# Seven half-size products for all tiles of 480 or 512 tokens, summed on in two PSUM banks and read in between

## The chip, the cores and the metric

The kernel runs on one core of a Trainium2 chip. Its engines are TensorE (PE in the profile; its weight loads are PEld), VectorE (DVE), ScalarE (ACT), GpSimd (POOL) and SyncE (SP), which here only issues transfers. The metric is the device time of one execution in microseconds. Three executions before the change took 838.07, 834.65 and 835.58 us: a median of 835.58 us.

## The reference, cut to what matters

An FFT mixer feeds a two-layer MLP. The input x is 8 sequences of 3008 tokens with 256 columns; the MLP is 256 to 2048 to 256.

```python
X = np.fft.rfft(x, axis=1)
Yr = Xr @ w_r - Xi @ w_i + b_r
Yi = Xr @ w_i + Xi @ w_r + b_i
lam = 0.01            # then both parts are shrunk towards 0 by lam
y = np.fft.irfft(Yr + 1j * Yi, n=x.shape[1], axis=1)

h = y @ w_in          # y as 24064 x 256, h 24064 x 2048
r = np.maximum(h, 0.0)
g = s * (r * r) + b
return g @ w_out      # 24064 x 256
```

## The kernel before, in words

**The FFT.** 3008 is taken as 94 x 32 (`N1`, `N2`), and the transform is done by small matmuls in stages: `s1_units` (the DFT over the 94, into the tile u), `s23_units` (the DFT over the 32, the mixing, the shrinking in the tile ring, and the inverse DFT into v) and `s4_units` (the inverse over the 94, into the tile yt, f16, 128 x 2 x 96 x 32). Between the stages the data goes out to DRAM and back in another order (ud, vd, issued on SP). Sequences 0 and 1 are done somewhat differently at the start, when the tables and weights are being loaded. All these stages leave PSUM through the two banks of the pool psf.

**The MLP.** The 24064 tokens are cut into 48 tiles (`_tile_order`): 12 "wide" ones for sequences 0 and 1 (512 or 480 tokens), then for each later sequence five "main" tiles of 512, and for each pair of sequences two "tail" tiles of 512 and 384 for the last 14 of the 94 rows. A tail's tokens are copied out of yt into the tile tail by POOL (L1036). For each tile `first_mm` makes h in 16 slots (`MC`); in each slot two matmuls of 512 columns (dc = 0, 1) fill one half of a two-bank tile psh, and after every second slot a relu (L1122 on ACT, L1124 on DVE) and a square (L1133 on ACT, L1135 on DVE) give a part of g in the tile gt. The sums with s and b come at the end, in the step that leaves PSUM.

**The second product** of a tile, g @ w_out, runs in the 16 slots of the tile after it, between that tile's first products. In `second_mms` it is 4 x 16 matmuls of 256 columns, in two banks of the pool psa, read by two DVE steps of 512 columns (L1234). In `seven_mms` the tile is cut into halves of tokens and of the inner dimension, the right side into halves of columns, and the 2 x 2 block product is done with seven block products instead of eight (Winograd's form): 7 x 16 matmuls of 128 columns. That asks for sums of blocks of w_out, made once (`make_t`, tile T_s), and for four sums of blocks of g for each half q of a tile (`s_op`): sums 1, 2 and 3 on DVE (L1276), sum 4 by an accumulating transfer that POOL issues (L1290). The seven products go to four banks, and nine DVE steps add them up through a tile zz (L1333, L1366). The function `seven` picks the tiles that are done so: 21 of the 48.

**The order of the work** is fixed by hand: every matmul is placed by the slots, and everything else is a "piece" (`later`) whose turn and engine stand in the table `TURNS`, two characters a piece: after how many matmuls it is issued, and on ACT, DVE, SP or POOL. Each engine works through its own queue in that order. `need` asserts that a piece has been issued before the matmul that depends on it; the waiting itself is done by semaphores.

Of the kernel before, what the change touches and what calls it, by code (L numbers as in the profile page):

```python
# [26 lines left out]
    "28292i242d21282g2l2q1w1x2h252i1o2h3e3m423m1k281k1o1o281t1h251k301h1s29202d371j3b251o21243h1s"  # L27
    "2k442l2q2y1c1d1h1g1p1t1w28202d21292t2x3m4a2u32181s1d1h1l1x21395i3y4i3a0w1s181c211k2c193m1e15"
    "1p21216a5u262u0s151g1t1d1h2h2h2q463m5u101g1s0w390x1h1p212l6q663m4y1g2c0l0t0k0o0y0x1t0w3d1x2e"
    "42190p1t1x292i4a4m560g5u0g0k1o0t0s102h1l4d85111l1x2d6i2y4y4e080e0c0k1h0s1s0t1d1d214a265u560c"  # L30
    "260t0w1g2d462m0h0o111k4k0x151h1p3e2a4u42045m0o0w1c0v0x0x191d1x292e3i2q3i0g0o380p3a101k1s3t42"
    "5e4q4y0l1d1x213h2x2d1t011y050c3c0d192d2t39393d350s4q040o0w0x16142k111h3e212d2l3q3e322i141d1c"
    "1m363m142c183m141d1k2w1s1t2h212y2e1h1q1c242p3d1x251w20252h2y1w201t2a1y2l2p1w3d1x271s3l20212f"
    "2129351k1o241w2t1x1y1w2s1w20242h21222h35202s1x251w20202g1x255a282k2l2x1p3i2y1q3i1d353t191h2w"
    "1c1c1l1p23141l1c39222l2r1l1p291k1s2t2035251w2021242d202g1z252h252d2l314e364q3a1c241l1t181g1w"
    "1l2t7f1l1s281t1t193q4m2u46263i2q0y292h0x11102s0x3l3t3x4q424q4y0d0r08100o1d1r0p0t1x112p141s1x"
    "0x0w25101g2w202l1b1x2h353t4m6i4q5e142l151x1k1u141c111k1o252d254232361y0x390x0o240w191l142t14"
    "1k2l1l1x2l2l462q4q4e0s4u145u18282d362i141g102h1121102k11144q11141l1k2t1w282c1h363e1l1p253p3y"
    "463m4e0j1g200x1a0s5214192o1h1g1g1k1d1k282x464y4i36151d1p1t3p3d41391t3t1p250d220o0y080k140t28"
    "195u182w1l21261x252x4232363a1c1g1l1o1g1m2q1t3e191p181o2g1o2c1p3a2q2y1g1u1d291t2h1o1w28282h25"  # L40
    "2e2028292e2m2l2x1s1w3s1t252f1s1w2x20292j1t25351k1o2o1w2t211u1w2s1t21252p2022393l1x1w3421211o"
    "211s201t234u1x24252p2d3e2q4a2q2h2x183g1515212f101910481y1c2d2n1l1p2h1c2d203g1l2d1x211s241x21"
    "252l2u323e3m1l1k2c3r1h291g2g1d1x1d1s212c301x252h2t323e423i171h1g202h2l193i363y4a3e2a3q460h0p"
    "0t0s1s101534141p1d1l1t313e3e3m3u1c2o0s3q1419212t3i152t11101t131g202c1g2d1x292l31363q3u361k1o"
    "1h4m1l1k1o2d4e191t1d1g211o284l1s211p1x212d2l3a2u3a42143e152c1012181l1c381t2y191o1s1y1w3c1t1x"
    "2d2h2l3x2p3l392h2p1x111024183u0v1l4q1p2g1k1p1x282t361k361l1p1y1o201d1y3a1t1x2g1x221s2529202c"
    "253u242a2e1w281x2l2t1x1x212a1o1w2d242c2t361x36292l1p2w1k1k292r1k1k3s1w2d2r1t1x2p1w1w281t291t"
    "2i252s1s25253420222d391x1w2s1x211s241x2g1w6n321x241x251x3i1y2x311o281l1x1l1z1g1t282p1q2d2n1t"
    "1t2l201k2l1w252t1o281t1w21282k1v252x2129313d4m3u3a3y1k1w151d1c1l1s1g215n1h1g1w1x2x1h2y3a212t"
    "1d1l182o1l3d4h4l4q5i564u111f0k2c0s1l1v11111918290o1d211h142x19181o1s21171x3l3t3x4m5u3u560s2k"  # L50
    "1h1l1042141d14181h15252d362m0o39110s300w1h3l101p141c3g1l212h3p464u463m0s4u181e15241x3m101415"
    "2c103t1c3g11155m1910391d1h1l1c1w2t361d1p1x314a3i3m2y0n1g1s105e185m151d2o191h181g1h1k2d353e1h"
    "1p21292l393x3l312h3d1x0k3q0x4i0c0g0o0o14195u1g2p1h1s1y1o20292y1h1s1w2t1t1u2q1p3i1p1t1s2s1s1w"
    "2s1t1u1y1o221p252d3p2028212525242a2028214u252p1t242s1o1x271s203t1x292n1t1t2d1s1s2h1p2x1t1u1s"
    "281w242c2l2c1y213p2424282d2d1t1x2429215j3q1w201t292d3e2i1p2x1c2k1g1p212j181l1c34262d2j1p1t2t"
    "1w1k2c1s2h291l2829292d24283n2h5p1x2l2l2t3q4m3a2u181k0x19101k1s1t2p131p1o241p1t212u32361u1t31"
    "1c1t1g3s1l393d3l4y4e3m3u191n0s141g1p1z11151x102x102g211l1c1k1t2930282h1r212l3l3t4i423q5a1829"
    "19191g421c1g191g1o1d3d1x3e2q0x2l11101o181d301g2x1d1s241t2h3l3t3y465q56184a154i1c1o2p3e101011"
    "1g112l0w280t0x3q0w0w18192p1l1o282x321d1l2l2t2y3m3m2y0n153d142614321c1g241l1o1p2k1w24313t461t"
    "1x1x214d392d2h313h391p0w3u0w4i0s1h0s10181c4q1k1w1h1t221t252d2y1k1s1s2t1s1u2m1p2m1o1t1s30291t"  # L60
    "24313e1y1x221s21252h1s2h1w1w28292i242d212a2h3120203s20212b211s2820252f2529351o252o1s2p211u1w"
    "2t1t24252w202224253825291s29202821274621252x2x252y321k2h1h1p1g1p1g2k5q1s1x2c1s2t1x2c1x1w2h1t"
    "241v2x3x2h461p1p1t2h4i422i2q101c101c1k192p47191g1s152i252x1d1h1k2o253h3l414u4y46520x1b0w2g14"
    "1p1z11152p1019101t2h1d1c2d1c1g281s2l1b253d3h494y665u46142c1d1l1942151819191k292x1p3m3a0k1h0x"
    "0w380x1c3l0w15191c1o1h1p1x2d364u2e52142q1d221g2o393m1c1g1h281l3p1g2h1d1h1q1h1l1w1k2t1w282l3h"
    "3m1l1x2h2t3e3y3i3m0n1g28141a1c4a1918241l1k1p2g1s20442d2m1p1t2h2t412t312p3h2x352d0o1m0o0y0l2x"
    "0w141w1p4y24281t252e2029393m1p1w1w281s1u2i202q1g251h2p1g1s212p2y3621321k2l1t211g1o2d1s2g242e"
    "212c252e2l2x1x202w1x252f1s1w3h212h2r1x1x2h1s1w2x1t2h1w1y202c2029283929222529202428292p1t2920"
    "2h20274e24242529213e26253l1o201s252d2n1l1l1s3c1i2h2n1l1t35201o2l1w292p1o241l242d242c2d5l1x2l"
    "2x393i4i3i3u1g1x1519181c1o1c2p1h1g1o212h193e2m2u3i253l0t1d0w2g1939414h52564i5a191n0k280o1p23"  # L70
    "0t112918350o1o2115152k101c341c1d1l3d414d4m565q560k241d1t0t1i0s1w0x1d1p212l2t2y3m0o2h110s0w14"
    "143g111t142t1l2d3h3l3y3m4a4i0x1m0w240x3a181g2015191g2c151k1o2x1p1x202c3d4a1p1t2529322q2a2y1c"
    "201d2q1h181t251s2t2124283d3m1t1x292h2x2d2l3t39392p2t11160o1c0w2t1l1s1g212e1w282l3e20242c1t22"
    "2i212o1x1x202d212e26282t25252425242828282p2y292x1t1s3g1s212f1o1w3l202p2z1t1x2h1k1o2t1l291o1w"
    "2t202424282128282s2525242h202o1x27242h21252h262e2029282928292828292h2539292i1s251w2920242t32"
    "2d2p1p2s1t1z1g2h1s351x272929292d1o2c1w2t2h3p1w2g1t1t1w2d202c2d391p3a1q212d1o281x271k2o202x21"
    "271x2d212t1x2d20202h351w2l1x251w20242c213l3p3q3y1x251l201p1z1c2g1o1t1l1r292t2x2x18211o1w1x20"
    "2d2l2025242d2539293i3m32221k1p1s1s1t1t1s1x202s2t2x1t221s1w1x2d20283p3u2d2h1s2k1p1z1k291s2l1p"
    "1z212t3h3h1g211s211s2c2x2x1o1o1p1s313d313i3619201c1l1k1p1o2c1p3e1o252425242524282126292m252i"
    "2122"  # L80
# [77 lines left out]
def kernel(  # L158
# [65 lines left out]
    zpool = ctx.enter_context(tc.tile_pool(name="zp", bufs=1))  # L224
# [273 lines left out]
    b_21 = cpool.tile([P, P], F32, name="b_21")  # L498
# [7 lines left out]
    def make_t(i):  # L506

        if not T_s:
            t_ops.append(later(
                lambda e: nc.vector.tensor_tensor(  # L510
                    out=b_21, in0=bias_bc[:, P:D], in1=bias_bc[:, 0:P], op=ALU.subtract
                ),
                {"dve": 0.2}, needs=bias_ops,
            ))
            T_s.append(x2pool.tile([P, 4, MC // 2, P], F16, name="T_s", tag="x2"))
        t = T_s[0]
        a, b, op = (
            (w_block(0, 1), w_block(0, 0), ALU.subtract),
            (t[:, 0], w_block(1, 1), ALU.subtract),
            (w_block(1, 1), w_block(0, 1), ALU.subtract),  # L520
            (w_block(1, 0), t[:, 1], ALU.add),
        )[i]
        t_ops.append(later(
            lambda e: nc.vector.tensor_tensor(out=t[:, i], in0=a, in1=b, op=op),
            {"dve": 0.6}, needs=t_ops[-1:],
        ))
# [476 lines left out]

    def s4_units(b):

        groups = []
# [4 lines left out]
        def unit(g):  # L1011
# [6 lines left out]
            for j in range(w):  # L1018
                h, k = divmod(n2 + j, HW)
                matmul(  # L1020
                    ps[:, j * N1 : (j + 1) * N1],
                    vs[(b, h)][:, k, ec * P : (ec + 1) * P], C_t[:, 0:N1],
                    start=True, stop=True,
                )

            done = leave_bank(
                yt[:, ec, 0:N1, n2 : n2 + w], ps,
                ps[:, 0 : w * N1].rearrange("p (j n) -> p n j", n=N1), w * N1,
            )
            y_ops[b].append((n2, w, done))  # L1030
            if g == len(groups) - 1 and b >= 2:
                pr, half = divmod(b, 2)
                if half == 0:
                    tails[pr] = tpool.tile([P, DC, 2, 14, N2], F16, name="tail", tag="tail")
                tail_copies[b] = later(
                    lambda e: nc.gpsimd.tensor_copy(  # L1036
                        out=tails[pr][:, :, half], in_=yt[:, :, 80:94, :]
                    ),
                    {"pool": 1.8}, needs=[op for _, _, op in y_ops[b]],
# [489 lines left out]
```

## Time and profile before

| | |
|---|---|
| median of three executions | 835.58 us |
| the profiled execution | 835.52 us |
| its span, first to last instruction | 833.7 us |
| PE busy | 818.9 us, 98% |
| DVE busy | 736.8 us, 88% |
| ACT busy | 702.2 us, 84% |
| POOL busy | 83.4 us, 10% |
| mean granted TensorE clock | 1.000 |
| mean busy share of the DMA engines, 100 to 750 us | 0.53 |

The span is what the profile covers; the execution's own time lies 1.8 us above it. A row of the profile names the source line, the engine, the operation, the tiles written and read, the shapes, how often it ran, the busy time, the mean duration of one, and how long its engine had been idle just before. The durations of neighbouring instructions on one engine overlap, since the end of one runs beside the start of the next, so starts are a better measure of pace than durations. A matmul's 128x512 is 128 rows of output by 512 columns.

### The profile page before, as it was taken

The page shows a single profiled execution, that of the slowest core. Times are in us where ns is not written, and L with a number is a line of the kernel's source. Part 1 is how long each engine was busy: PE and PEld are TensorE (multiplying, and loading weights), DVE is VectorE, ACT ScalarE, POOL GpSimd, SP SyncE. Part 2 cuts the span into 40 slices and gives each one's busy share as a digit, 9 for nine tenths or more (in the row PEclk, how much of TensorE's full clock was granted, in tenths as well). Part 3 has the DMA queues.
Part 4 walks back from the last instruction along what each step waited for, and adds up shares of the span by engine and source line. Part 5 has one row for each costly group of instructions (what it writes and reads, how often), then busy time and mean ns, then how long its engine had stood idle before and what let it go on. Part 6 is the DMA issues. An engine that isn't in the chain of part 4 may idle for free.

```text
span 833.7 us, 19076 instructions
## 1 busy us (share of the span) xinstructions
PE 818.9 (98%) x7662; PEld 598.5 (72%) x7662; DVE 736.8 (88%) x1192; ACT 702.2 (84%) x874; POOL 83.4 (10%) x112
## 2 busy tenths in 40 slices
PE   7999999999999999999999999999999999999997
PEld 6857777777677767777677766777667777767765
DVE  5988989997898999998899979999989989889984
ACT  5989889989798889888889988897879987878774
POOL 4630000100011000110001100110001000001000
PEclk9999999999999999999999999999999999999999
DMA  8963546664547367454656545654566333513222
GB/s 202 182 170 82 120 138 171 131 129 123 173 114 166 85 176 188 108 118 128 176 141 161 112 124 150 150 130 116 129 177 149 72 92 96 140 45 77 74 49 77
DMA packets 114929, 107.14 MB, mean 129 GB/s; under 512 B 11036, under 2 KB 99104, under 8 KB 113496
## 3 DMA queue, kind: packets, MB, share of 16 engines
q1 hardware_dynamic: 100760, 80.55, 33.2%
q0 software_dynamic: 14080, 25.37, 18.5%
q8 instruction: 60, 0.98, 0.5%
q14 instruction: 29, 0.24, 0.1%
HBM read 53.52 MB, written 46.66 MB: 120 GB/s over the span
## 4 chain that ended last, share of the span: by engine, by line
PE 83%; DVE 8%; DMA 5%; ACT 2%; issue 1%; POOL 0%; SPq 0%; DVEq 0%; ACTq 0%; POOLq 0%
PE psh L234 34%; PE psa L234 31%; PE psf L234 17%; DMA ring<-ring 2%; DMA gt<-gt 2%; DVE rt L1124 1%; DMA x<-in_x_dram 1%; PE psm L234 1%; DVE gt L1135 1%; ACT rt L1122 1%; DVE u L297 1%; DVE yt L297 1%; DVE gt L1276 1%; DVE ring L934 0%; POOL x L370 0%
## 5 line engine op out<-in xcount | busy, mean ns | idle before, releaser
L234 PEld LDWEIGHTS <-gt 128*128 128x128 f16 (+1 forms) x3696 | 305.1, 101 | 168.9 <-DMA gt<-gt 1.1
L234 PE MATMUL psh<-yt,w_in 128*128 128x512 f16 (+1 forms) x1344 | 397.2, 378 | 1.5 <-ACT u L297 0.8
L1122 ACT ACTIVATE rt<-psh 128x1024 f32<-128x1024 f32 (+2 forms) x310 | 311.4, 1006 | 63.1 <-PE psh L234 55.7
L234 PE MATMUL psa<-w_out_t,gt 128*128 128x256 f16 (+3 forms) x2448 | 310.1, 253 | 0.7 <-DMA gt<-gt 0.6
L1133 ACT ACTIVATE gt<-rt 128x1024 f16<-128x1024 f32 (+2 forms) x254 | 261.6, 1041 | 11.4 <-DVE rt L1124 8.6
L1135 DVE TENSOR_TENSOR gt<-rt 128x1024 f16<-128x1024 f32 (+2 forms) x130 | 154.3, 1194 | 7.7 <-ACT rt L1122 7.0
L234 PEld LDWEIGHTS <-w_in 128*128 128x128 f16 x1536 | 136.3, 98 | 25.2 <-issue 3.2
L1124 DVE TENSOR_SCALAR rt<-psh 128x1024 f32<-128x1024 f32 (+2 forms) x74 | 88.2, 1193 | 19.9 <-PE psh L234 17.5
L1290 POOL DMA_DIRECT2D gt<-gt x42 | 38.1, 907 | 505.5 <-DVE gt L1276 231.6
L234 PE MATMUL psa<-T_s,gt 128*128 128x128 f16 (+1 forms) x944 | 79.6, 219 | 0.3 <-DVE zz L1333 0.3
L890 DVE TENSOR_TENSOR ring<-psf,s 128x512 f16<-128x512 f32 x84 | 57.6, 686 | 19.9 <-PE psf L234 11.1
L234 PE MATMUL psh<-tail,w_in 128*128 128x512 f16 (+1 forms) x192 | 52.1, 353 | 0.0
L234 PEld LDWEIGHTS <-xf 128*128 128x128 f16 x504 | 47.1, 98 | 4.9 <-DVE xf L850 0.5
L234 PE MATMUL psf<-W_g,xf 128*128 128x256 f16 x336 | 50.4, 273 | 0.0
L297 ACT CAST yt<-psf 128x470 f16<-128x470 f32 (+2 forms) x60 | 37.1, 646 | 4.4 <-PE psf L234 4.2
L1234 DVE SCALAR_TENSOR_TENSOR ost<-psa,s_bc,bias_bc 128x512 f32<-128x512 f32 (+2 forms) x51 | 36.9, 723 | 3.0 <-PE psa L234 2.9
L234 PE MATMUL psf<-x,A_t 94*96 94x512 f16 x102 | 38.9, 382 | 0.3 <-DVE u L297 0.2
L297 ACT CAST xf<-psf 128x512 f16<-128x512 f32 x52 | 30.3, 585 | 10.1 <-PE psf L234 9.9
L1333 DVE SCALAR_TENSOR_TENSOR ost<-psa,s_bc,zz 128x256 f32<-128x256 f32 (+1 forms) x80 | 36.6, 477 | 1.6 <-PE psa L234 0.8
L234 PE MATMUL psf<-C_t,vs 96*128 96x94 f16 (+1 forms) x484 | 37.7, 205 | 0.3 <-ACT yt L297 0.3
L297 ACT CAST u<-psf 96x512 f16<-96x512 f32 x54 | 31.0, 578 | 6.7 <-PE psf L234 5.4
L297 ACT CAST v<-psf 128x512 f16<-128x512 f32 x49 | 28.6, 583 | 9.3 <-PE psf L234 9.1
(121 smaller groups left out, 890.8 us busy)
## 6 DMA issues: line engine op xcount, KB each, us to landing
out_dram<-ost SPq DMA_DIRECT2D x65, 256.0 KB
ud<-u SPq DMA_DIRECT2D x56, 192.0 KB
us<-ud SPq DMA_DIRECT2D x28, 384.0 KB
vd<-v SPq DMA_DIRECT2D x42, 256.0 KB
vs<-vd SPq DMA_DIRECT2D x14, 768.0 KB
x<-in_x_dram POOLq DMA_DIRECT2D x28, 376.0 KB, 6.4
gt<-gt POOLq DMA_DIRECT2D x38, 256.0 KB, 4.0
ring<-ring SPq DMA_DIRECT2D x120, 64.0 KB
```

Of the source, the lines that this page charges most:

```text
L234: return nc.tensor.matmul(out, lhs, rhs, **how)
L297: (nc.scalar.copy if e == "act" else nc.vector.tensor_copy)(out=dst, in_=src)
L890: lambda e: nc.vector.tensor_tensor(out=ring[0][:, i % 4], in0=ps, in1=hold[i // 2][:, i % 2].unsqueeze(1).to_broadcast([P, 2, D]), op=ALU ...
L1122: nc.scalar.activation(out=rt, in_=ps[:, :, 0:w], func=AF.Relu)
L1124: nc.vector.tensor_scalar(out=rt, in0=ps[:, :, 0:w], scalar1=0.0, scalar2=None, op0=ALU.max)
L1133: nc.scalar.activation(out=gt, in_=rr, func=AF.Square)
L1135: nc.vector.tensor_tensor(out=gt, in0=rr, in1=rr, op=ALU.mult)
L1234: nc.vector.scalar_tensor_tensor(out=osts[number % 3][0:size, 0:k], in0=ps[0:size, 0:k], scalar=s_bc[0:size], in1=bias_bc[0:size].unsqueez ...
L1276: nc.vector.tensor_tensor(out=out, in0=a, in1=b, op=op)
L1290: nc.gpsimd.dma_start(out=a12, in_=a11, accum_op=ALU.add)
L1333: nc.vector.scalar_tensor_tensor(out=out, in0=of, scalar=s_bc[0:size], in1=other, op0=ALU.mult, op1=ALU.add)
```

## The change

All tiles of 480 or 512 tokens from tile 4 to tile 45 use `seven_mms`: 39 tiles instead of 21. The rest (tiles 0 to 3, the three of 384 tokens, and the last two) stay with `second_mms`.

Inside `seven_mms` the seven products now use two banks instead of four. Three places of 256 columns are used, called x, v and y: products 0, 4, 5 and 2 all go to x and are added on top of each other, product 1 goes to v, and products 3 and 6 to y; v and y share a bank. The running sums are read between the products by seven DVE steps of 256 columns, a, g, b, c, e, f and h, straight into the output tile ost; zz, `b_21` and the step L1366 are gone. A product that adds to a place must wait until the reading step of that place is done: 4 waits for a, 5 for b, 2 for c, 6 for e, and 3 for g. The order of the products becomes 0, 1, 4, half of 3, 5, the other half of 3, 2, 6, with uneven numbers of matmuls in the slots. Sum 4 may be made on DVE too.

The tile yt of sequences 2 to 7 is kept in 12 blocks of 8 n1, each as 32 x 8, so that a step of `s4_units` writes runs of eight values; its matmuls take 96 columns instead of 94. The rows of a main tile stand in another order for that, and `store` sends them to the same places in DRAM in the same number of pieces for main tiles, and in more and smaller ones for the three tiles of 384. The tail is moved by a transfer issued on SP instead of a copy by POOL. `TURNS` is a new table.

```diff
 TURNS = (
...
 )
...
-    zpool = ctx.enter_context(tc.tile_pool(name="zp", bufs=1))
...
-    b_21 = cpool.tile([P, P], F32, name="b_21")
...
+    def in_blocks(b):
+
+        flat = yts[b].rearrange("p e m n -> p e (m n)")
+        return flat.rearrange("p e (k n r) -> p e k n r", k=12, n=N2)
+
     def s4_units(b):
 
+        cols = N1 if b < 2 else 96
...
+            if b < 2:
+                dst = yt[:, ec, 0:N1, n2 : n2 + w]
+                src = ps[:, 0 : w * N1].rearrange("p (j n) -> p n j", n=N1)
+            else:
+                dst = in_blocks(b)[:, ec, :, n2 : n2 + w].rearrange("p k j r -> p j k r")
+                src = ps[:, 0 : w * 96].rearrange("p (j k r) -> p j k r", j=w, k=12)
+            done = leave_bank(dst, ps, src, w * cols)
...
                 tail_copies[b] = later(
-                    lambda e: nc.gpsimd.tensor_copy(
-                        out=tails[pr][:, :, half], in_=yt[:, :, 80:94, :]
+                    lambda e: nc.sync.dma_start(
+                        out=tails[pr][:, :, half].rearrange("p e k t -> p e (k t)"),
+                        in_=in_blocks(b)[:, :, 10:12].rearrange("p e k n r -> p e (k n r)"),
                     ),
-                    {"pool": 1.8}, needs=[op for _, _, op in y_ops[b]],
+                    {"sp": 0.6}, needs=[op for _, _, op in y_ops[b]],
                 )
...
-            return yts[b][:, dc, 16 * j : 16 * j + 16, :]
-        return tails[b][:, dc].rearrange("p h m n -> p (h m n)")[:, j : j + w]
+            return in_blocks(b)[:, dc, 2 * j : 2 * j + 2].rearrange("p k n r -> p (k n r)")
+        if j == 0:
+            return tails[b][:, dc, :, 0]
+        return tails[b][:, dc, :, 1].rearrange("p h (n r) -> p h n r", r=8)[:, :, :, 0:6]
...
+            rows = out[row : row + 256].rearrange("(r h n) d -> n r h d", r=8, h=2)
+            send(rows[:, :, half : half + k], src[:, 0:k])
...
+            if n == 4 and e == "pool":
+                nc.gpsimd.dma_start(out=a12, in_=a11, accum_op=ALU.add)
+                return
             out, a, b, op = {
                 1: lambda: (s1(), a21, a22, ALU.add),
                 3: lambda: (a21, a11, a21, ALU.subtract),
                 2: lambda: (a11, a11, s1(), ALU.subtract),
+                4: lambda: (a12, a12, a11, ALU.add),
             }[n]()
...
-        firsts = (0, 2, 3, 5)
         sum_of = {3: 1, 4: 2, 5: 3, 6: 4}
...
+        place = "xvxyxxy"
+        ops = {}
+
         def mm(n, j, c):
...
+            if (n, j, c) in ((0, 0, 0), (1, 0, 0)):
+                bank = sum_bank(ti)
+                two = bank.rearrange("p (n j e) -> p n j e", n=2, j=2)[0:size]
+                hold["x" if n == 0 else "v"] = two[:, 0]
+                hold["xb" if n == 0 else "yb"] = bank
+                if n:
+                    hold["y"] = two[:, 1]
...
+            before = {4: "a", 5: "b", 2: "c", 6: "e", 3: "g"}.get(n)
+            if before and j == 0 and c == 0:
+                need([ops[before]])
...
+            m = matmul(
+                hold[place[n]][:, j], lhs, right[n][:, c],
+                start=(n in (0, 1) and j == 0 and c == 0), stop=(c == C - 1),
                 skip_group_check=True,
             )
...
+            if name == "a":
+                add("a", o(0, 0), "x", bias(0), needs=new_o(0))
+            elif name == "g":
+                add("g", o(0, 0), "v", o(0, 0), needs=[ops["a"]])
+            elif name == "b":
+                add("b", o(0, 1), "x", bias(1), needs=[ops["a"]])
+            elif name == "c":
+                add("c", o(1, 1), "x", bias(1), needs=new_o(1))
+            elif name == "e":
+                add("e", o(1, 1), "y", o(1, 1), needs=[ops["c"]])
+            elif name == "f":
+                add("f", o(1, 0), "x", bias(0), needs=[ops["e"]])
+                store(tl, 2, 2, hold["o", 1], ops["f"])
             else:
...
+                add("h", o(0, 1), "y", o(0, 1), needs=[ops["b"], ops["g"]])
+                store(tl, 0, 2, hold["o", 0], ops["h"])
...
+        put(0, qs=(0,))
+        put(1, qs=(0,))
+        put(0, qs=(1,))
+        put(1, qs=(1,))
+        put(4)
+        put(3, js=(0,))
+        put(5)
+        put(3, js=(1,))
+        put(2)
+        put(6)
...
+        for k in (6, 6, 6, 6, 8, 8, 8, 8, 8, 8, 8, 8, 8, 6, 5, 5):
...
     def seven(ti):
-        if ti >= len(tiles) - 2 or not halves(ti):
-            return False
-        firsts = [mark[b] // MC for b in range(2, B)]
-        return (
-            ti >= firsts[-1] or 4 <= ti < 7 or any(m - 2 <= ti < m for m in firsts)
-            or any(ti == mark[b] // MC for b in range(3, B - 1))
-        )
+        return 4 <= ti < len(tiles) - 2 and halves(ti)
...
-                if mc == 10 and seven(ti):
+                if mc == 11 and seven(ti):
                     own_sums(ti, 0)
```

## The prediction

> **What bounds the kernel now.** I read the page's busy times and chain first, then the rows by shape, the waits of PE, and the order in time at a few places.
>
> ```profile
> span 833.7 us, 19076 instructions
> PE 818.9 (98%) x7662; PEld 598.5 (72%) x7662; DVE 736.8 (88%) x1192; ACT 702.2 (84%) x874; POOL 83.4 (10%) x112
> PE 83%; DVE 8%; DMA 5%; ACT 2%; issue 1%; POOL 0%; SPq 0%; DVEq 0%; ACTq 0%; POOLq 0%
> ```
>
> PE is busy throughout, and 83% of the chain is PE. A busy PE need not be a full one, so the pace decides. The order in time shows the second product beside the first, plain at 307 us and in seven at 795 us:
>
> ```profile
> 306.83 0.59 PE L234 MATMUL psh<-yt,w_in 128*128 128x512 f16 x2
> 307.27 0.60 PE L234 MATMUL psa<-w_out_t,gt 128*128 128x256 f16 x4
> 307.70 0.38 PE L234 MATMUL psh<-yt,w_in 128*128 128x512 f16 x1
> ...
> 795.07 0.55 PE L234 MATMUL psf<-w_out_t,gt 128*128 128x128 f16 x7
> 795.46 0.59 PE L234 MATMUL psh<-yt,w_in 128*128 128x512 f16 x2
> ```
>
> From start to start, four products of 256 columns take 0.43 us and seven of 128 take 0.39. Over all neighbours of one shape in the trace the medians are 109 ns, 56 ns, and 216 ns for 512 columns: or 2.4 columns per ns ((512 - 128) / (216 - 56)) and 3 ns for each matmul. So PE runs without gaps, and its time is its columns. All waits of PE for others between 60 and 790 us:
>
> ```profile
> PE psf L234 <- DMA ring<-ring: 1.3, 2, 0.8
> PE psf L234 <- ACT yt L297: 0.6, 2, 0.3
> PE psa L234 <- DMA gt<-gt: 0.6, 2, 0.4
> PE psa L234 <- DVE zz L1333: 0.3, 1, 0.3
> PE psf L234 <- DVE ring L890: 0.3, 1, 0.3
> ```
>
> That is 3.1 us in 730; its weight loads show 2.8 more with a named releaser. Beside PE, DVE and ACT are nearly full (busy times by stretch, columns PE, PEld, DVE, ACT, POOL):
>
> ```profile
> 100.00:750.00 650.00, 646.94 (x5993) 470.72 (x5991) 587.64 (x943) 560.49 (x686) 48.81 (x61) 1.00 0.53 132
> 439.00:472.00 33.00, 33.00 (x361) 24.99 (x358) 31.51 (x60) 32.59 (x40) 5.99 (x8) 1.00 0.64 140
> 622.00:655.00 33.00, 33.00 (x398) 24.97 (x396) 31.64 (x56) 31.48 (x40) 4.42 (x5) 1.00 0.48 123
> ```
>
> Over two tiles (33 us) both stood at 95 to 99% and PE lost nothing. The question is whether that can be held.
>
> **The change part by part**, against the profiled execution's 835.5 us (span 833.7 and 1.8 around it), which is 0.06 below the median of the runs.
>
> *PE columns.* 18 more tiles go from 64 products of 256 columns to 112 of 128: 64 x 0.109 - 112 x 0.056 = 0.70 us each (0.64 by the rounded lines above), all on the path: **-12.7** (-11.5 to -12.7). In s4_units, 384 matmuls grow from 94 to 96 columns, 41 to 43 ns: **+0.5** (0.3 to 0.8).
>
> The Trainium skill, page "TensorE: Matmul & The Clock Gate", section "Back-to-back issue gap", says that in a real stream of weight loads and matmuls a 128-column one takes about 81 ns, not 56. By that estimate a tile would take 112 x 0.081 = 9.1 us instead of 7.0, and the kernel about 873 us. The trace disagrees: 0.39 us for seven.
>
> *DVE.* Reads: 273 steps (39 x 7) at 0.477 = 130.2, for 147 x 0.477 + 21 x 0.746 + 21 x 0.433 = 94.9: +35.3. Sums: three per half tile, 42 to 78 of each, and by the new table 4 of the 78 fourth sums on DVE: 112 x 0.683 = +76.4. Plain reads (L1234): 36 fewer at 0.744, -26.8. The table takes away 24 relus (-28.9), 26 squares (-31.3) and 18 copies of u, 6 of v (and adds one of s), and yt's balance is +2.0: -13.6 in all. Without `b_21`, in sum **+11** of 736.8.
>
> *ACT.* 26 squares more (+27.1), 24 relus (+24.3), u, v and s +13.3; yt -8.9: **+55.8** of 702.2. A yt step of the new layout has no row; the old one ranges from 0.553 (470 columns) to 0.838, mean 0.683. Runs of eight values are nearer to the plain copies of 512 columns (0.583), so I take 0.56 for 480; at 0.68 ACT has 5 us more.
>
> By tile, the last seven lose 13 us of DVE and gain 6 of ACT. So 100 to 750 us, shortened by 12 to 638, gets 588 + 24 = 612 of DVE and 560 + 50 = 610 of ACT, both 96% (overlaps counted double, so rather less). That is the load of the two 33-us stretches, in all stages from tile 7 on. Such stretches lost 0.06 to 0.5 us each by the gaps between matmuls; 12 of them over 390 us, at 0.1 above the usual: **+1** (0 to 6).
>
> *The reads in between.* Four of the seven reads of a tile (a, b, c, h) must fit beside 8 small matmuls and what stands with them. Counting the matmuls in the instruction order at the paces above, the time from the last matmul into a place to the next one into it is 1.10 us at the shortest and 1.5 to 1.75 in the middle; g, e and f have 1.9 or more. Before, psa's shortest was 1.95. Needed are the matmul's own tail (219 - 56 ns) and the read, 0.477: 0.64. A slack of 0.46 to 1.1 us is short beside a DVE square of 1.22. But psf's banks live so already: 91 of their turns after 60 us are under 1.8 us, and the waits of PE for ACT and DVE above are 1.2 us: 0.013 each. For 156 reads **+2.0** (0 to 8, at 0.05 each). DVE too must have sum 2 of the second half ready within 1.9 us, since product 4 now comes third; this is inside the same bound.
>
> The Trainium skill, page "Perfetto Trace Analysis", section "Matmuls", advises to rotate independent matmul groups through different PSUM banks, so that emptying one lies beside the next group. This change goes against it; the sum by that advice would be the second case below. The short turns of psf speak for the milder price.
>
> *Sum 4 by transfer.* 42 to 74 issues on POOL, 0.907 us each: +29 us on a POOL that is 10% busy, minus 6.5 for the tail copies. Their time to landing is 3.2 to 8.8 us, and product 6 comes 5.0 us at the soonest and 9.3 in the middle after the issue (6.3 and 8.9 before). PE and its weight loads waited 1.7 us for 42: **+1.3** for 32 more (0 to 3). They also load the DMA engines: 256 KB each, by bytes some 6 points on 0.53; the ring moves, for which PE and its loads waited 2.3 us, land a little later: **+0.5** (0 to 2).
>
> *The tail.* POOL's copy ran into DVE: an add of 0.28 us took 1.68 while POOL copied, and 2.4 us later PE waited for zz.
>
> ```profile
> 342.78 1.68 DVE L850 TENSOR_TENSOR xf<-xf 128x256 f16<-128x256 f16 x1
> ...
> 343.04 1.26 POOL L1036 COPY tail<-yt 128x896 f16<-128x896 f16 x1
> ```
>
> Two of the other five copies stretched a DVE step by 0.35. Gone: **-0.3** (-0.5 to 0). On SP come 6 transfers, waiting for the last yt step, and 12 output pieces; behind them on SP stand ring, u and v. SP waits hundreds of us in all for its producers, so this is inside the ring's 0 to 2.
>
> Sum: -12.7 + 0.5 + 1 + 2.0 + 1.3 + 0.5 - 0.3 = **-7.7**, so **827.8 us**. With all terms at their best 822.6; with all at their worst (-11.5 + 0.8 + 6 + 8 + 3 + 2) 843.8.
>
> **Other ways it could go.**
>
> *The reads come late (slower).* Place: product 4, 5 or 2 behind a, b or c, product 1 of the next tile behind h. If DVE has just begun a 1.22 us square when a place is full, the read ends 1.6 us later, 0.5 beyond the shortest gap. One read in five so: 31 x 0.5 = 15.6 instead of 2.0, **841 us**. The gain is gone at 0.062 us per read on the mean, and it is 0.5% slower from 0.09. For it: DVE is in order, and no PSUM place is free meanwhile. Against it: psf's 0.013.
>
> *ACT and DVE can't be held at 96%.* The best 50 us of DVE stood at 93.9% (46.9 busy). If that is the ceiling for long stretches, the middle takes 612 / 0.939 = 652 instead of 638, 841 us; but busy times overlap by about 0.085 us per instruction (a square of 1.22 is followed after 1.13), and 89 are added: 604 / 0.939 = 644, **833 us**. For it: the stretches above 95% were short. Against: they lost nothing.
>
> *Small products don't keep their pace.* If each paid its weight load's 98 ns row, a tile would take 11.0 us instead of 7.0: 835.5 + 18 x 4.0 = **908 us**. The 21 tiles that already do it exclude this nearly.
>
> **How the numbers follow.** A measurement of this kernel tells about 0.5%, 4.2 us, from no change: under 831.4 is faster, over 839.8 slower. The forecast has 0.66, its own range 822 to 831. Late reads 0.20, of which 0.06 within 0.5% and 0.14 beyond; the ceiling 0.13, of which 0.11 within; the pace 0.01. So faster 0.66, same 0.17, slower 0.17. The range leaves out 0.03 below 822 and 0.17 above: to 837.
>
> **What will show it.** Right: seven 128-column matmuls in 0.39 us in all tiles, DVE busy near 748 and ACT near 758, PE's waits for ost steps below 4 us in all, no DVE add above 1 us. The second case shows as waits of PE psa for DVE ost, tens of them of 0.2 to 0.6 us; the third as PE psh waiting for relus and squares at ACT over 96%. The prediction is wrong if the gaps between matmuls add more than 12 us.

## The result: 862.3 us instead of the 827.8 forecast

The changed kernel takes 862.26 us (median), the kernel before 835.99 us beside it. The ratio is 1.034, with a 95% interval of 1.031 to 1.037. The forecast of 827.8 us missed by 34.5 us and named the wrong side.

The page of the changed kernel, its span, busy times, the queue that carries the sum-4 transfers, and the shares of the chain:

```profile
span 859.8 us, 21103 instructions
PE 818.1 (95%) x8526; PEld 603.0 (70%) x8526; DVE 740.5 (86%) x1281; ACT 749.8 (87%) x944; POOL 106.9 (12%) x138
q0 software_dynamic: 19072, 33.74, 24.2%
PE 48%; DMA 10%; DVE 7%; ACT 5%; issue 2%; POOL 0%; SPq 0%; DVEq 0%; ACTq 0%
gt<-gt POOLq DMA_DIRECT2D x69, 256.0 KB, 4.6
```

DVE at 740.5 and ACT at 749.8 us are some 8 us below the 748 and 758 forecast. What is new is the chain. It can be followed back only to 227 us here, so its shares add up to 72% of the span, but of these DMA has 10 and PE 48, where in the kernel before DMA had 5 and PE 83 of 99. The queue q0 went from 18.5% to 24.2%, which is the 6 points that the prediction worked out. The median transfer of sum 4 lands 4.6 us after its issue; by the same row it was 4.0 us before.

What PE waited for in the changed kernel (us in total, times, longest):

```profile
PE psa L237 <- DMA gt<-gt: 21.9, 7, 5.5
PE psf L237 <- DMA ring<-ring: 3.2, 2, 2.0
PE psa L237 <- DVE ost L1362: 1.4, 4, 0.6
PE psf L237 <- DMA vs<-vd: 0.4, 2, 0.3
```

Seven waits for transfers of sum 4 make 21.9 us, where the kernel before had 0.6 and the prediction added 1.3. The reads between the products, the risk to which it gave most room, cost 1.4 us.

The second loss is the clock. These are stretches of the changed kernel (columns: the stretch and its length, busy time of PE, PEld, DVE, ACT, POOL, granted clock of PE, share of the DMA engines, GB/s):

```profile
209.00:215.00 6.00, 1.65 (x16) 0.83 (x12) 4.03 (x11) 2.28 (x3) 0.00 (x0) 0.92 1.01 197
215.00:222.00 7.00, 6.69 (x40) 4.41 (x41) 1.98 (x3) 3.80 (x6) 0.00 (x0) 0.58 0.02 6
231.00:238.00 7.00, 2.84 (x30) 1.82 (x29) 4.01 (x6) 3.57 (x5) 0.00 (x0) 0.99 1.03 259
238.00:242.00 4.00, 4.00 (x27) 2.36 (x25) 0.79 (x2) 1.81 (x3) 0.00 (x0) 0.58 0.30 90
535.00:542.00 7.00, 4.70 (x28) 3.00 (x29) 0.64 (x2) 1.73 (x3) 0.00 (x0) 0.52 0.39 105
```

PE stands still while the DMA engines are full (shares of 1.01 and 1.03), and in the stretch right behind it runs at about half the clock, with the DMA engines at 0.02 to 0.39. The trace holds five such episodes besides the run's end: 6.83, 3.41, 6.83, 3.41 and 3.41 us at a granted clock of 0.5, from 214, 238, 535, 624 and 740 us on. In these 23.9 us PE works for 20.2; the rest is the end of waits that are counted above. Half of the 20.2 is lost, 10.1 us. The kernel before had no such episode. Four of the five stand behind long waits for sum 4, the one from 624 us on behind the wait of 2.0 us for a ring move. So 20.0 us of waits for sum 4 over the forecast (21.9 - 0.6 - 1.3) and 10.1 of clock make 30.1 of the 33.9 us by which the profiled execution (861.7 us) is over the forecast. The waits for ring moves, 3.2 us instead of 1.3, are part of the rest.

**Why the transfers are late.** The new table puts the two transfers of a tile on POOL in the reversed order in 18 tiles, the second half's ahead of the first half's (the recorded expectations count 17). In the kernel before this happens in none. POOL works in order, and product 6 reads the first half first. The order in time of the changed kernel at the second product of tile 9; a selection of DVE, POOL, SP's queue and PE (start, duration, instruction, and in brackets the idle time before it):

```profile
223.45 0.68 DVE L1297 TENSOR_TENSOR gt<-gt,s 128x1024 f16<-128x1024 f16 x1
225.50 0.69 DVE L1297 TENSOR_TENSOR gt<-gt,s 128x1024 f16<-128x1024 f16 x1
226.82 1.76 POOL L1289 DMA_DIRECT2D gt<-gt  x2 [20.22 <-DVE ost L1362]
227.91 1.59 SPq L977 DMA_DIRECT2D vs<-vd  x1
232.75 0.59 PE L237 MATMUL psh<-yt,w_in 128*128 128x512 f16 x2
237.50 0.51 PE L237 MATMUL psa<-w_out_t,gt 128*128 128x128 f16 x6 [4.16 <-DMA gt<-gt]
```

The two DVE lines are sum 2 of the first and of the second half. The first half's transfer could have left soon after 224.13, when its sum was done. It left only at 227.36, behind the second half's, whose sum was done at 226.19, and right after the two a load of vs of 768 KB was issued. The trace gives 5.4 and 10.1 us from issue to landing for the two. The second figure is the first half's, and PE waited 4.16 us for it. So the reversed order does two things at once: the first half's transfer leaves some 3 us later, and it lands behind another one, some 5 us later after its issue. Six of the seven long waits lie at tiles with the reversed order (8, 9, 17, 22, 24 and 26). The seventh, at tile 38, is of the same kind: one half's sum 4 is on DVE there, and the transfer of the other goes late, beside a load of vs.

The Trainium skill, page "DMA: Bandwidth & Descriptors", section "Two DMAs through the same engine are not ordered", says that within one queue of one DMA engine descriptors start in order. The landings of the pair above are in keeping with it, as the transfer issued first landed some 5 us earlier, but a landing does not show a start.

### The profile page after: what moved, and what is told of

The parts are those of the page before. It is cut to its first block, busy times and chain, and to the rows that moved or that the text cites. A ratio compares the mean times of both kernels' runs of the same rounds, so it can differ in the third digit from the quotient of the medians.

```text
span 859.8 us, 21103 instructions
## 1 busy us (share of the span) xinstructions
PE 818.1 (95%) x8526; PEld 603.0 (70%) x8526; DVE 740.5 (86%) x1281; ACT 749.8 (87%) x944; POOL 106.9 (12%) x138
## 3 DMA queue, kind: packets, MB, share of 16 engines
q0 software_dynamic: 19072, 33.74, 24.2%
## 4 chain that ended last, share of the span: by engine, by line
PE 48%; DMA 10%; DVE 7%; ACT 5%; issue 2%; POOL 0%; SPq 0%; DVEq 0%; ACTq 0%
PE psh L237 21%; PE psa L237 17%; PE psf L237 11%; DMA gt<-gt 7%; ACT rt L1134 2%; ACT gt L1145 2%; DMA vs<-vd 2%; DVE ost L1362 2%; DMA ring<-ring 2%; DVE gt L1297 1%; ACT u L300 1%; DVE ring L886 1%; DVE s L1297 1%; DVE v L300 1%; DMA out_dram<-ost 0%
## 5 line engine op out<-in xcount | busy, mean ns | idle before, releaser
L237 PE MATMUL psa<-w_out_t,gt 128*128 128x128 f16 (+3 forms) x2224 | 218.3, 232 | 22.2 <-DMA gt<-gt 21.9
L1147 DVE TENSOR_TENSOR gt<-rt 128x1024 f16<-128x1024 f32 (+2 forms) x104 | 123.9, 1200 | 6.6 <-ACT rt L1134 5.6
L237 PE MATMUL psa<-T_s,gt 128*128 128x128 f16 (+1 forms) x1680 | 128.0, 219 | 1.2 <-DVE ost L1362 1.1
L1362 DVE SCALAR_TENSOR_TENSOR ost<-psa,s_bc,ost 128x256 f32<-128x256 f32 (+1 forms) x117 | 55.9, 478 | 28.3 <-PE psa L237 28.0
L1362 DVE SCALAR_TENSOR_TENSOR ost<-psa,s_bc,bias_bc 128x256 f32<-128x256 f32 (+1 forms) x140 | 67.0, 479 | 11.5 <-PE psa L237 9.5
L1136 DVE TENSOR_SCALAR rt<-psh 128x1024 f32<-128x1024 f32 (+2 forms) x50 | 59.6, 1191 | 12.1 <-PE psh L237 7.0
L1297 DVE TENSOR_TENSOR gt<-gt 128x1024 f16<-128x1024 f16 (+1 forms) x82 | 55.7, 680 | 0.4
L1297 DVE TENSOR_TENSOR gt<-gt,s 128x1024 f16<-128x1024 f16 (+1 forms) x78 | 53.3, 683 | 1.8 <-PE psa L237 1.0
L237 PEld LDWEIGHTS <-s 128*128 128x128 f16 (+1 forms) x624 | 41.8, 100 | 17.5
L1297 DVE TENSOR_TENSOR s<-gt 128x1024 f16<-128x1024 f16 (+1 forms) x78 | 53.1, 681 | 0.9 <-ACT gt L1145 0.3
L237 PE MATMUL psa<-T_s,s 128*128 128x128 f16 (+1 forms) x624 | 47.6, 219 | 0.0
```

What stands on the lines that cost most here:

```text
L237: return nc.tensor.matmul(out, lhs, rhs, **how)
L1136: nc.vector.tensor_scalar(out=rt, in0=ps[:, :, 0:w], scalar1=0.0, scalar2=None, op0=ALU.max)
L1147: nc.vector.tensor_tensor(out=gt, in0=rr, in1=rr, op=ALU.mult)
L1297: nc.vector.tensor_tensor(out=out, in0=a, in1=b, op=op)
L1362: ins = nc.vector.scalar_tensor_tensor(out=out(), in0=hold[of], scalar=s_bc[0:size], in1=other(), op0=ALU.mult, op1=ALU.add,)
```

## The experiments

Theory 1 was the late order and the half clock behind it. Rival 1 was that 74 transfers load the DMA engines too much, whatever their order. Rival 2 was that the reads and the nearly full DVE and ACT cost the time.

**The order put right.** When POOL's turn comes for a second half whose first half has not gone, the two change places.

```diff
+    swapped = {}
...
-            begin(pieces[k], engine)
+            op = swapped.pop(id(pieces[k]), pieces[k])
+            first = getattr(op, "first", None)
+            if first is not None and not first.gone and engine == "pool":
+                swapped[id(first)] = op
+                op = first
+            begin(op, engine)
...
+        if n == 4 and q == 1:
+            sum_ops[(ti, n, q)].first = sum_ops[(ti, n, 0)]
```

> The changed kernel with one thing altered: where the order of turns issues the sum-4 transfer of a tile's second half ahead of that of its first half (17 tiles), the two change places, so that the first half's always goes first; same instructions, same number of transfers. Theory 1 (the 26 us are sum-4 transfers that land after product 6 wants them, mostly because the first half's stands behind the second half's on POOL and on the queue, and the half clock that follows each long stop of PE): six of the seven long waits go, PE's waits for gt transfers fall from 21.9 us to about 6, one half-clock episode is left of five, so 834 us (829 to 840). Rival 1 (74 transfers are simply too much for the DMA engines, whatever their order): 855 to 862. Rival 2 (the reads between the products and DVE and ACT at 96% cost the time, the waits for transfers only replace them): 855 to 862 with the waits moved to DVE and ACT steps.

Measured: 838.5 us, 1.004 of the kernel before (1.002 to 1.006). PE's waits in this kernel:

```profile
PE psf L237 <- DMA ring<-ring: 4.4, 2, 2.6
PE psf L237 <- DMA vs<-vd: 4.1, 3, 2.5
PE psa L237 <- DVE ost L1370: 3.1, 5, 1.9
PE psa L237 <- DMA gt<-gt: 0.8, 1, 0.8
```

The order alone gave back 23.8 us. That covers the 18 tiles and also tile 38, where the edit trades the halves: POOL moves the first one and DVE adds the second. The waits for sum 4 fell from 21.9 to 0.8 us, and no half-clock episode is left in the profiled execution (mean clock 0.998; the other nine had 0.991 to 0.996, so some of them may still have had one). But 838.5 is not the 834 of theory 1 (829 to 840): the waits for ring and vs moves, and for ost steps, rose from 5.0 to 11.6 us. Before the longest of the ost waits (1.9 us) DVE itself stood still for 2.45 us, with no engine named; what such a step still needs is that its buffer has been stored, so this is probably a transfer too. Something of rival 1 is left.

**Nobody reads the sum; and no transfer at all.** The first edit leaves every transfer but lets product 6 read another part, the second drops the transfers.

```diff
-        left = [(0, 0), (0, 1), (1, 1), None, (0, 0), (1, 0), (0, 1)]
+        left = [(0, 0), (0, 1), (1, 1), None, (0, 0), (1, 0), (1, 1)]
```

> The changed kernel, with product 6 reading the part a22 instead of the part that sum 4 is added into; every transfer is made at the same place with the same bytes, but no product reads what it brings (product 6 is so computed from other data of the same size). Theory 1: no wait for gt transfers, no half clock but perhaps after a wait for a ring transfer, so the forecast of the prediction without its transfer term, 826 to 830 us. Rival 1 (the load of the transfers slows the rest): waits for ring moves and loads grow, 845 or more. Rival 2 (reads and loaded engines): 850 or more, with PE waiting for DVE and ACT.

```diff
             if n == 4 and e == "pool":
-                nc.gpsimd.dma_start(out=a12, in_=a11, accum_op=ALU.add)
                 return
```

> The changed kernel without the 74 sum-4 transfers (that sum is left out, product 6 reads the part without it; the 4 sums on DVE stay). Theory 1: as the kernel whose transfers nobody reads, within 2 us of it: 825 to 829 us. Rival 1 (load): clearly faster than that kernel, by 10 us or more. Rival 2: 850 or more, as DVE, ACT and the reads are as they were.

Measured: 839.1 us with the transfers unread (1.005, 1.002 to 1.007) and 825.5 us without them (0.988, 0.986 to 0.990). The first lies between the expectations of theory 1 (826 to 830) and rival 1 (845 or more). The unread kernel's two largest waits, and then the page of the kernel without transfers:

```profile
PE psf L237 <- DMA ring<-ring: 8.1, 3, 3.8
PE psf L237 <- DMA vs<-vd: 4.0, 4, 2.3
```

```profile
span 825.0 us, 20795 instructions
PE 807.6 (98%) x8526; PEld 598.6 (73%) x8526; DVE 738.6 (90%) x1281; ACT 748.2 (91%) x944; POOL 38.9 (5%) x64
q0 software_dynamic: 6496, 14.42, 11.1%
```

So theory 1 alone is wrong. The transfers cost 13.6 us even if nobody reads them, since ring and vs moves land later beside them: PE waits 12.1 us for these moves instead of 2.1, and two windows of 3.41 us at half clock follow such waits instead of one. The 13.6 us are as much as the swapped kernel has over the kernel without transfers (13.0 us). Rival 2 is out: without the transfers DVE and ACT do the same work, the reads are where they were, and the time is 825.5 us. That is where the prediction's sum stands without its two transfer terms (827.8 - 1.3 - 0.5 = 826.0).

Two stretches show the load, each first in the swapped kernel and then in the kernel without transfers (columns as above). With the transfers the share of the DMA engines is higher, and PE, which was busy throughout, stands still for 2 to 2.5 us:

```profile
230.00:260.00 30.00, 27.46 (x340) 21.31 (x339) 24.95 (x44) 26.59 (x35) 3.56 (x4) 1.00 0.73 180
230.00:260.00 30.00, 29.98 (x369) 23.63 (x367) 27.34 (x51) 29.14 (x39) 0.00 (x0) 1.00 0.43 124
590.00:620.00 30.00, 28.11 (x288) 19.76 (x286) 27.66 (x51) 27.45 (x36) 3.98 (x5) 1.00 0.83 192
590.00:620.00 30.00, 29.96 (x330) 21.18 (x330) 28.84 (x52) 28.63 (x36) 0.00 (x0) 1.00 0.61 165
```

**The transfer as early as it can be.** Instead of at its turn, each transfer enters POOL's order as soon as its sum 2 has entered DVE's.

```diff
...
+            for op in [op for op in fourths if all(n.gone for n in op.needs)]:
+                fourths.remove(op)
+                if engine_of[op.at] == "pool":
+                    begin(op, "pool")
...
```

> The changed kernel with each sum-4 transfer put into POOL's order as soon as its sum 2 has been put into DVE's and product 1 has been put into PE's, instead of at its turn of the table: the halves go in order and product 6 comes 6.2 us of PE's work at the soonest and 10.0 in the middle after the issue, instead of 5.0 and 9.3. Theory 1: as the swap or 1 to 3 us better, 827 to 836 us, waits for gt transfers 2 to 6 us. Rival 1 (load): 855 to 862. Rival 2: 855 to 862.

Measured: 840.8 us (1.006, 1.003 to 1.008). That is above the expectation, and not told apart from the swap (1.002 to 1.006). Tile by tile it is better than the swap at some places and worse at others: against the kernel without transfers, the tile behind tile 38 is 4.6 us longer again. There this edit leaves the second half on POOL, as in the changed kernel, while the swap traded the halves: PE waits 3.6 us for a transfer that lands 10.2 us after its issue, and the clock is at half for 6.83 us. So what the lead alone is worth stays open.

**The kernel before, with the order reversed.** Its table and its 42 transfers are kept; in each tile POOL holds the first half's until the second half's has gone.

```diff
...
+            op = pieces[k]
+            if getattr(op, "held", False):
+                continue
             begin(op, engine)
+            first = getattr(op, "first", None)
+            if first is not None:
+                begin(first, engine)
...
```

> The kernel before, with only this altered: in all of its 21 tiles in seven products POOL issues the sum-4 transfer of the second half first and that of the first half right behind it, instead of the first half's some 2.5 us ahead. Same 42 transfers, same bytes. Product 6 then comes 4.9 us of PE's work at the soonest and 7.0 in the middle after the issue, instead of 6.3 and 8.9. Theory 1 (the order of the halves costs by itself): PE's waits for gt transfers grow from 0.6 us to between 5 and 20, with one to three half-clock windows, 840 to 855 us. Rival 1 (only the number of transfers counts): 834 to 837.

Measured: 846.5 us, 1.013 (1.011 to 1.014). PE's largest wait there, which was 0.6 us in the kernel before:

```profile
PE psa L234 <- DMA gt<-gt: 6.1, 7, 3.4
```

The order costs 11 us by itself, in a kernel where nothing else is changed: 6.1 us in these waits, 1.7 us by one half-clock episode of 3.41 us behind the longest, and some 3 us in small waits that are not assigned here. As in the changed kernel, the first half's transfer also leaves later (some 2.5 us), so this too is the price of both things together.

**The load taken away where it is highest.** In the swapped kernel, six tiles whose transfers run beside x, vs and ring moves do sum 4 otherwise: on DVE, or not at all, with product 6 made on both parts.

```diff
+        if n == 4 and ti in (8, 9, 10, 12, 26, 31):
+            sum_ops[(ti, n, q)].only = "dve"
...
```

> The swapped kernel, with sum 4 of six tiles (8, 9, 10, 12, 26, 31) as an add on DVE at the same turns: 12 transfers fewer, in the stretches where the swapped kernel still lost time against the one without any transfer (195 to 330 us, 520, 603). Rival 1 in its narrower form (what is left of the loss, 13 us, is the transfers' load beside x, us, vs and ring moves in those stretches): stops for vs, ring and stores there fall from about 11 us to under 5; DVE takes 12 x 0.68 = 8 us more, mostly beside PE: 829 to 836. If DVE is the bound there: 840 to 847. If it is not those stretches: 838 to 840.

```diff
...
+        if ti in TWICE:
+            order[-16:] = [
+                (n, j, c) for q in range(2) for n in (6, 7) for j in range(2)
+                for c in range(4 * q, 4 * q + 4)
+            ]
...
-        right = [w_block(0, 0), w_block(1, 0), T[:, 3], T[:, 0], T[:, 1], T[:, 2], w_block(1, 1)]
+        right = [w_block(0, 0), w_block(1, 0), T[:, 3], T[:, 0], T[:, 1], T[:, 2], w_block(1, 1), w_block(1, 1)]
...
```

> The swapped kernel, with no sum 4 in the same six tiles: product 6 is made on both parts (16 matmuls of 128 columns more, 0.9 us, six times). Rival 1 in its narrower form: the same stops fall to under 5 us, PE takes 5.4 us more, DVE nothing: 833 to 837. If it is not those stretches: 843 to 846.

Measured: 828.4 us on DVE (0.992, 0.990 to 0.995), and 830.2 us with the doubled product (0.994, 0.992 to 0.996). Two edits that share only the 12 transfers they leave out gain 10.1 and 8.3 us, a little more than was expected of either, so it is the load in those stretches. The first was run once more, in five rounds:

> The swapped kernel with sum 4 of the same six tiles on DVE once more, as it was the fastest that computes everything: 826 to 831 us, 0.989 to 0.995 of the kernel before.

Measured: 826.3 us, 0.989 (0.988 to 0.991). This computes everything and beats both kernels. Its page, and its largest waits:

```profile
span 824.0 us, 21091 instructions
PE 807.7 (98%) x8526; PEld 599.1 (73%) x8526; DVE 744.7 (90%) x1293; ACT 748.3 (91%) x944; POOL 94.3 (11%) x126
```

```profile
PE psm L237 <- DMA x<-in_x_dram: 2.9, 5, 0.8
PE psa L237 <- DVE ones L386: 1.0, 1, 1.0
PE psf L237 <- DVE u L306: 1.0, 2, 0.8
```

The first two are the start of the run. No wait for sum 4, ring or vs is among the largest.

**How far DVE could take it.** All 78 fourth sums on DVE, or those of 14 tiles.

> The changed kernel with every sum 4 as an add on DVE at its turn of the table and no transfer: 74 x 0.683 = 50.5 us more on a DVE that is busy 739 of 825 us without them. If DVE were already at its ceiling (the prediction's second rival), all of it would show: 870 us or more. If DVE has the room that its busy share leaves and only the stretches at 96% have none: 835 to 855 us, with PE waiting for DVE's steps and no half clock to speak of.

> The swapped kernel with sum 4 on DVE in 14 tiles (7 to 14, 25, 26, 31 to 33 and 38) instead of six: 16 x 0.683 = 11 us more on DVE than with six. If the transfers' load is still what is left: 825 to 828 us and the runs closer together. If DVE's room is used up: 830 to 838 us.

Measured: 847.2 us with all (1.014, 1.012 to 1.017) and 831.8 us with 14 tiles (0.996, 0.994 to 0.998). The kernel with all of them:

```profile
PE 815.5 (96%) x8526; PEld 597.3 (71%) x8526; DVE 777.6 (92%) x1355; ACT 750.1 (89%) x944; POOL 39.7 (5%) x64
PE 56%; DVE 30%; issue 5%; DMA 4%; ACT 3%; POOL 0%; SPq 0%; DVEq 0%; ACTq 0%; POOLq 0%
```

The 74 adds are 50.5 us by their rows, and DVE's busy time grows by 39.0, since neighbours overlap. Of that, 21.6 us show against the kernel without the sum; DVE has 30% of the chain there. The first 12 sums cost next to nothing (826.3 and 828.4 against 825.5), and with 14 tiles the kernel takes 3 to 5.5 us longer than with six, in the range expected if DVE's room is used up. So DVE had some room, and the transfer was the right idea for most sums.

**Order and load, two prices or one.** The changed kernel with its reversed order, but with those six tiles on DVE.

> The changed kernel with sum 4 of the six tiles (8, 9, 10, 12, 26, 31) on DVE and without the swap: 13 tiles are left in which the second half's transfer goes first, all outside the stretches where the DMA engines are fullest. If order and load are two separate prices (24 and 10 us): 847 to 853. If the order costs its long stops only where the load is high too (tiles 8, 9 and 26): 834 to 841, the waits for gt transfers at 5 to 9 us (those of tiles 17, 22, 24 and 38 in the profile of after), one half-clock window at most.

Measured: 842.4 us, 1.008 (1.007 to 1.010), between the two expectations. PE waits 10.7 us for sum 4, and the clock is at half twice for 3.41 us:

```profile
PE psa L237 <- DMA gt<-gt: 10.7, 5, 3.4
```

Four kernels make a table (us):

| | order of the table | first half first |
|---|---|---|
| all transfers | 862.3 | 838.5 |
| six tiles on DVE | 842.4 | 826.3 (and 828.4) |

The order costs 24 us with the full load and 14 to 16 without it. The load of those six tiles costs 20 us with the bad order and 10 to 12 with the good one. The difference of 8 to 10 us does not show that the two make each other dearer: four of the six tiles (8, 9, 10 and 26) were among the 18 with the reversed order, so the lower row also has the reversed order in fewer tiles, 14 (the recorded expectation counts 13). In the changed kernel tiles 8, 9 and 26 alone had 14.3 us of the waits. What is shown is that the order costs 14 to 16 us outside the fullest stretches too (with tile 38, whose wait is 3.3 us here), so that the second expectation, that it costs its long stops only where the load is high, was wrong.

**The clock by itself.** PE does bursts of 94 to 96 matmuls of 512 columns (some 20 us), and between them waits for ACT, which copies a varied width.

```python
for turn in range(3):
    for n in WIDTHS:                       # 512 to 3584
        for i in range(BURST + turn):      # 94
            ps = banks.tile([P, 512], F32, name="ps", tag="ps")
            nc.tensor.matmul(ps, w, rhs if i == 0 else x16, start=True, stop=True)
        nc.scalar.copy(out=s[:, 0:512], in_=ps)
        nc.scalar.copy(out=d[:, 0:n], in_=s[:, 0:n])
        rhs = d[:, 0:512]
```

> Nothing of the reference is computed: 39 bursts of 94 to 96 matmuls of 512 columns, some 20 us each, and between them PE stands still for 1.3 to 4.2 us, while ACT copies 512 to 3584 columns; each length three times, against other points of the clock's grid. Theory A, read from the rows of the kernels run so far (the clock is set for the next 3.41 us by how much PE worked in the 3.41 us before, on a grid that runs freely, and it falls to half where that was under some 0.4): stops under 2.0 us never lower the clock, those of 2.1 to 4 us do so or not by where they lie on the grid, those above some 4.1 us always do. Theory B (the length of the stop alone decides, with a threshold of 3.4 us): all three of a length go the same way.

There were 38 stops between bursts. These stretches are cut on the clock's grid of 3.413 us, with the same columns as above:

```profile
94.44:97.86 3.42, 2.02 (x10) 0.96 (x10) 0.00 (x0) 1.31 (x2) 0.00 (x0) 1.00 0.00 0
97.86:101.27 3.41, 3.41 (x18) 1.52 (x17) 0.00 (x0) 0.00 (x0) 0.00 (x0) 1.00 0.00 0
...
715.67:719.08 3.41, 1.39 (x8) 0.59 (x7) 0.00 (x0) 1.84 (x2) 0.00 (x0) 1.00 0.00 0
719.08:722.50 3.42, 3.42 (x10) 1.22 (x9) 0.00 (x0) 0.00 (x0) 0.00 (x0) 0.50 0.00 0
545.00:548.42 3.42, 1.55 (x8) 0.59 (x6) 0.00 (x0) 1.75 (x2) 0.00 (x0) 1.00 0.00 0
548.42:551.83 3.41, 1.98 (x10) 0.91 (x10) 0.00 (x0) 1.38 (x1) 0.00 (x0) 1.00 0.00 0
551.83:555.24 3.41, 3.41 (x17) 1.53 (x16) 0.00 (x0) 0.00 (x0) 0.00 (x0) 1.00 0.00 0
```

The stops near 94 and 716 us are of one length (2.18 us). The first straddles two windows of the grid, and the clock stays. The second lies in one window, PE is busy for 1.39 of 3.41 us in it, and the next window runs at 0.50: 10 matmuls instead of 18. The stop at 546 us is longer (3.46 us), but is split so that PE is busy for 1.55 and 1.98 us in its two windows, and the clock stays. Counting 216 ns for each matmul from its start, the clock fell behind all 14 stops with a window that was busy for 0.39 of its length or less, and behind none of the 24 others, whose emptiest window was 0.40 or more. By length: none of 9 stops under 2.0 us, 9 of 24 between 2.1 and 3.7, all 5 above 3.8. Theory A holds, theory B falls.

## Why the prediction was wrong, step by step

- *PE columns, s4, the reads in between, the tail: right in sum.* Without the transfers the kernel takes 825.5 us where these terms make 826.0. That it is within 0.5 us is in part luck, for the terms were not measured one by one, and the trace of that kernel has a wait of 1.9 us for vs and a window of 3.41 us at half clock that no term stood for. The loads of DVE and ACT came out at +3.7 and +47.6 us in the changed kernel instead of +11 and +55.8, with no cost to be seen. In the changed kernel no wait for a read of ost is over 0.6 us, and no add of L850 (now L846) is over 0.3 us with POOL's copy gone. The rivals on the reads, the ceiling of ACT and DVE and the pace of small products did not happen. The ceiling rested on 93.9% as DVE's best 50 us, but that was the best of stretches cut at multiples of 50: from 322 to 372 us of the kernel before DVE was busy for 49.4 of 50 us.
- *The step that failed is "Sum 4 by transfer", +1.3 us (0 to 3).* It took the waits of 42 transfers in the kernel before and scaled them to 74. It did look at the lead of product 6 over the issue (5.0 us at the soonest), but not at which half goes first. The new table reverses that in 18 tiles, and this, with tile 38, costs 24 us: 21.9 us of waits for sum 4, and the half clock behind them. Beside a landing of 3.2 to 8.8 us in the rows, a lead of 5.0 us was no cover for a transfer that stands behind another. The instruction order of POOL would have shown it; I counted POOL's issues and did not pair them.
- *The load on ring moves, +0.5 us (0 to 2), was mis-sized.* It is 13 us (838.5 against 825.5). I took the share of the DMA engines over most of the run (0.53, some 6 points more). The transfers meet x, us, vs and ring moves in short stretches in which the DMA engines are full (1.01 and 1.03 in the lines above, over 6 and 7 us of the changed kernel), and a mean does not show those.
- *A term is missing.* A stop of PE of some 2 us can cost another 1.7 us by the clock, and more when the window behind it is not busy enough either (2.8 and 2.2 us here). In the changed kernel that made 10.1 us. I had read the clock of the kernel before, found 1.00, and left it there.
- The range (822 to 837) put nothing on transfers beyond 5 us, so even its slow side was a case of DVE, not of DMA.

The description of the kernel says that the table's number tells after how many matmuls a piece is issued. In the code it is the number of places that the piece goes back in the queue of pieces, which is how two pieces of a tile can change places on POOL.

## What to carry to other kernels

When an order of work is replaced, compare for each queue not only how many instructions it issues but in which order the halves of one job leave, against the order in which they are read; the price is the later issue and the landing behind the other one. Judge added transfers by the fullest stretches that they fall into, since a mean share of 0.6 hides stretches at 1.0, and test the load apart from the wait by letting the transfers run unread. Where DVE still has a little room, a few sums moved back there, in the fullest stretches only, were worth 10 us, while with all of them moved the kernel was 9 us slower than with none moved (847.2 against 838.5).

## What the runs showed of the hardware

The granted clock of PE is set on a grid of 3.413 us: in all traces here every change lies a whole number of windows from the others. In the changed kernel, for example, the stretches at the full clock last 208.21, 17.07 and 293.55 us, which are 61, 5 and 86 windows, and those at half 3.41 or 6.83, one or two. A window in which PE works for less than about 0.4 of it puts the next one at half. In the traces of the kernels that run the whole FFT and MLP, with each matmul counted from its start at its pace at the full clock (56 ns for 128 columns, 109 for 256, 216 for 512) even in a half-clock window, the windows before a half-clock one were busy for 0.00 to 0.39 (once 0.45, by a count that lacks matmuls that the trace may have lost), and those of 0.40 or more, that case aside, were not followed by one. So a stop of 2.18 us can lower the clock, and one of 3.67 us need not.

The Trainium skill, page "TensorE: Matmul & The Clock Gate", says in "What's actually happening" that the window is 3413 ns and runs freely, with which the traces agree. In "HAM oscillation — how this bites in real kernels" it gives the rule "no PE-idle gaps >~3.4µs". Here the measurement decides against that figure: stops of 2.18 to 3.25 us lowered the clock 8 times in 18, and what decided was the busy share of a window.

A further surprise was how exact the rest is: between the swapped kernel and the one without transfers, 34 of 47 tiles take the same time to 0.01 us, and nearly the whole difference lies in the other 13. A table of tile times against the kernel without transfers finds every place where something comes late.
